# Attention followed by a gated product: the same steps in another order, with 59 visits to parts of the array instead of 84

## The chip, the cores and the metric

The kernel runs on one core of one Trainium2 chip. The time is device microseconds of one launch, the median of several runs; less is better. TensorE (PE) multiplies, VectorE (DVE), ScalarE (ACT) and GpSimd (POOL) do the element-wise work, and SyncE (SP) issues every DMA.

## The reference

Band attention with a few global tokens, followed by a gated linear layer. There are 8 batches, 8 heads, 512 local and 32 global tokens, heads 64 wide. All is float32.

```python
k_all, v_all = [k_g, k_l], [v_g, v_l]                     # joined along the tokens
out_g = sm(q_g @ k_all.T / 8) @ v_all                     # global queries see every key
s_ll  = where(abs(i - j) <= 32, q_l @ k_l.T / 8, -1e9)    # local queries: a band of 32 to each side
out_l = sm([q_l @ k_g.T / 8, s_ll]) @ v_all               # and the 32 global keys
x     = [out_g, out_l] as (8 * 544 tokens) x 512
out   = ((x @ w1) * (x @ w2)) @ w3 @ w_out                # w1, w2: 512 x 1024, w3: 1024 x 1024, w_out: 1024 x 512
```

## The kernel before

**Attention.** The work of a batch is cut into four head pairs, so there are 32 pairs m = 0 to 31, eight groups of four. For each pair the steps are: `s` (scores, line 349), 64 small matmuls that each use 64 rows and 32 columns of the array; `mm` (line 356) and `ex` (line 361), mask, minimum and exponential on DVE and ACT; the probabilities P are turned, for m < 4 by PE, for all others by DVE (line 369) with four DMAs out to DRAM (line 375) and one back in as Pt (line 380); `v` (line 399), 64 small matmuls on 128 rows and 32 columns; `nm` (line 415) divides by the sums; the result goes through PE (m < 4) or through DRAM (lines 432 and 436) into token order, and `xh` and `xl` (lines 439 and 442, the output tile is x) split it into a high and a low part in a reduced float32 type, in two halves e = 0, 1 of the tokens. The global queries of two pairs go together as one of 16 quads u: `sg` (line 466, array parts of 64 x 32), softmax, DMA out and in (Gd, Gt), `vg` (line 502, parts of 128 x 32, and line 505), `gn` (lines 510 to 512), `gb` (line 515) and so on. A step `s`, `v`, `sg` or `vg` is called a group below, and a stretch of groups between matmuls that use the whole array (128 x 128) is called a visit to parts of the array.

**Gated product.** The tokens are taken in 17 pieces k of 256, each in four quarters n. A quarter has four `first` steps (lines 548 to 550), each 12 matmuls of 128 x 256, that fill the PSUM tiles ap and bp (one buffer each); gates: `ga` copies ap to as, `gb_` (line 558) multiplies bp by it, `gh` and `gl` (lines 439 and 442, one buffer each) split the product; then two `second` steps (lines 578 to 580), each six matmuls of 128 x 512, add to acc; `out` and `store` (line 594) end a piece.

**Weights.** SP fetches w1, w2, w3 and w_out (line 650, three raw buffers); DVE and ACT unpack them (lines 606, 608, 610) and split w12 into w12h and w12l (lines 439 and 442); PE multiplies w3 by w_out in 64 `fold` steps (line 686). K and V of a pair are loaded by line 282 and lines 290 to 296; `vs` (line 305) shifts the copies of V for the first four pairs, `kc` (line 325) and `vc` (line 315) write the global keys and values into K and V.

**Order.** Nothing is scheduled at run time. A table, ORDER_OF (lines 39 to 187), holds a number for each step, and a letter A, D or P where a step may run on ACT, DVE or POOL. The steps are issued in the order of these numbers, and each engine and the one DMA queue of SP run their own in that order. An engine whose next step has to wait holds up all that stands behind it on that engine.

```python
    for n, (key, on) in enumerate(steps):
        word = next(words[key[0]])
        out.append((int(word.lstrip("ADP")), n, letters[word[0]] if word[0] in letters else on[0]))
    out.sort()
```

Of the kernel before, what the change touches and what calls it, by code (L numbers as in the profile page):

```python
# [26 lines left out]
LAG, TP, LATE, VC = 1, 4, 4, 4  # L27
# [71 lines left out]
    tp="181 179 233 236 297 300 354 357",  # L99
    pt="A186 A187 A237 A241 A302 A305 A359 A362",  # L100
    v="205 245 311 367 471 592 697 740 823 884 938 1013 1091 1127 1231 1267 1365 1403 1512 1540 1640 1677 1786  "
    "1814 1914 1951 2062 2090 2190 2225 2332 2360",
    iv="131 219 301 358 422 503 632 706 760 833 890 952 1024 1098 1188 1240 1324 1373 1463 1528 1598 1647 1737 1803  "
    "1871 1921 2011 2079 2147 2197 2284 2350",
    nm="213 249 316 376 494 628 703 750 828 887 948 1019 1094 1137 1237 1275 1369 1410 1517 1545 1643 1686 1791  "
# [953 lines left out]
```

## Time and profile before

| | |
|---|---|
| time, median of 3 runs (lowest to highest) | 813.24 us (806.35 to 817.27) |
| the profiled execution: its time, its span | 811.82 us, 810.0 us |
| mean granted clock of TensorE | 0.981 |
| PE busy with matmuls | 768.9 us (95% of the span) |
| PEld (weight loads of PE) | 668.7 us (83%) |
| DVE, ACT, POOL busy | 440.9 us (54%), 308.2 us (38%), 103.3 us (13%) |
| chain that ended last, share of the span | PE 72%, DMA 14%, DVE 6%, SP's queue 3% |
| DRAM read and written over the span | 169 GB/s |

Busy times are sums of instructions on an engine. Matmuls are pipelined, so PE's busy time tells when it had nothing to do, not how well it was used. "Granted clock" is the share of full speed at which TensorE was allowed to run. In a timeline an idle time stands in brackets, with what ended it; small matmuls of one group stand in one row.

### The profile page before, as it was taken

What the parts mean: (1) busy time and instruction counts of PE and PEld (TensorE: products, weight loads), DVE (VectorE), ACT (ScalarE), POOL (GpSimd) and SP (SyncE); (2) the same over time, 40 slices, a digit from 0 to 9 for tenths busy, and PEclk for the clock granted to TensorE, in tenths of its full rate; (3) what the DMA queues carried; (4) which work ended last, traced back from release to release, by engine and by line L of the source; (5) the groups of instructions that cost most, each with busy time, mean ns of one, the idle gap of its engine ahead of it and who ended that gap; (6) DMA issues with size and microseconds to landing.
All of it is one profiled execution on the core that took longest, in us unless ns stands there. A gap on an engine that the chain in (4) does not pass through costs nothing.

```text
span 810.0 us, 25385 instructions
## 1 busy us (share of the span) xinstructions
PE 768.9 (95%) x10564; PEld 668.7 (83%) x10564; DVE 440.9 (54%) x1371; ACT 308.2 (38%) x938; POOL 103.3 (13%) x142
## 2 busy tenths in 40 slices
PE   6799898989999999999999999999999998999995
PEld 3245587879999989999989999899989988989994
DVE  3777788757465556565645555555465655431121
ACT  2677745334344333333424242425242523211111
POOL 1121221103020011110101010101010101000000
PEclk8999999999999999999999999999999999999998
DMA  7878786868676557675756676757665567410000
GB/s 226 274 246 239 190 210 217 222 189 229 199 211 175 165 163 187 187 197 164 217 152 167 173 201 172 195 155 207 179 185 156 157 174 200 117 49 27 1 27 27
DMA packets 97467, 138.23 MB, mean 171 GB/s; under 512 B 15272, under 2 KB 57896, under 8 KB 97352
## 3 DMA queue, kind: packets, MB, share of 16 engines
q1 hardware_dynamic: 97352, 136.60, 59.7%
q8 instruction: 83, 1.36, 0.7%
q14 instruction: 32, 0.26, 0.1%
HBM read 96.71 MB, written 39.85 MB: 169 GB/s over the span
## 4 chain that ended last, share of the span: by engine, by line
PE 72%; DMA 14%; DVE 6%; SPq 3%; issue 2%; ACT 1%; POOL 1%; DVEq 0%; ACTq 0%; POOLq 0%
PE bp L548 8%; PE acc L578 7%; PE acc L579 6%; PE bp L549 6%; PE acc L580 6%; PE bp L550 6%; PE ap L548 6%; PE ap L549 6%; PE ap L550 6%; DMA Gt<-Gd 4%; PE v L399 4%; PE w L686 3%; PE s L349 3%; DMA raw_w<-in_w_t_dram 2%; PE gx L502 2%; DMA K<-in_kp_t_dram 2%
## 5 line engine op out<-in xcount | busy, mean ns | idle before, releaser
L548 PE MATMUL bp<-x,w12h 128*128 128x256 f32 x512 | 151.7, 296 | 1.2 <-DVE gl__1361 L442 0.8
L548 PE MATMUL ap<-x,w12h 128*128 128x256 f32 x512 | 146.4, 286 | 0.1
L549 PE MATMUL ap<-x,w12h 128*128 128x256 f32 x512 | 144.2, 282 | 0.0
L549 PE MATMUL bp<-x,w12h 128*128 128x256 f32 x512 | 144.2, 282 | 0.0
L550 PE MATMUL bp<-x,w12l 128*128 128x256 f32 x512 | 144.1, 281 | 0.0
L550 PE MATMUL ap<-x,w12l 128*128 128x256 f32 x512 | 143.8, 281 | 0.0
L361 ACT ACTIVATE P<-P,mn 128x128 f32<-128x128 f32 x256 | 99.7, 391 | 36.8 <-DVE mn L356 30.1
L548 PEld LDWEIGHTS bp<-x,w12h 128*128 128x128 f32 x512 | 97.7, 191 | 10.0 <-issue 5.0
L548 PEld LDWEIGHTS ap<-x,w12h 128*128 128x128 f32 x512 | 97.4, 190 | 6.9 <-issue 1.0
L549 PEld LDWEIGHTS ap<-x,w12h 128*128 128x128 f32 x512 | 97.7, 191 | 4.3
L550 PEld LDWEIGHTS ap<-x,w12l 128*128 128x128 f32 x512 | 98.3, 192 | 0.0
L550 PEld LDWEIGHTS bp<-x,w12l 128*128 128x128 f32 x512 | 97.8, 191 | 0.0
L549 PEld LDWEIGHTS bp<-x,w12h 128*128 128x128 f32 x512 | 97.6, 191 | 0.2 <-issue 0.2
L356 DVE CUSTOM_DVE_ANT_0 P<-s,cs 128x128 f32<-128x128 f32 x256 | 58.1, 285 | 31.9 <-PE s L349 31.9
L686 PE MATMUL w<-wo,w3f 128*128 128x512 f32 x128 | 63.0, 631 | 10.7 <-DVE wo L610 6.7
L315 POOL COPY V<-vg 32x1024 f32<-32x1024 f32 x40 | 44.7, 1138 | 172.0 <-PE gx L505 143.3
L686 PEld LDWEIGHTS w<-wo,w3f 128*128 128x128 f32 x128 | 23.6, 197 | 41.0 <-issue 21.8
L361 ACT ACTIVATION_READ_ACCUMULATOR P<-P,mn 128x1 f32 x256 | 48.1, 188 | 0.0
L325 POOL COPY K<-K 128x480 f32<-128x480 f32 x40 | 24.4, 616 | 173.4 <-DMA K<-in_kp_t_dram 144.6
L490 ACT ACTIVATE G<-G,mg 128x256 f32<-128x256 f32 x64 | 32.0, 501 | 34.9 <-DVE mg L484 17.5
L349 PE MATMUL s<-K,q 64*32 64x128 f32 x2048 | 38.0, 277 | 3.3 <-POOL K L325 3.0
L399 PE MATMUL v<-V,Pt 128*32 128x64 f32 x2048 | 36.2, 223 | 4.9 <-DMA Pt<-Pd 2.9
(789 smaller groups left out, 1377.4 us busy)
## 6 DMA issues: line engine op xcount, KB each, us to landing
Pd<-P SPq DMA_DIRECT2D x112, 128.0 KB
Pt<-Pd SPq DMA_DIRECT2D x28, 512.0 KB
raw_w<-in_w_t_dram SPq DMA_DIRECT2D x24, 512.0 KB
V<-in_v_t_dram SPq DMA_DIRECT2D x64, 192.0 KB
K<-in_kp_t_dram SPq DMA_DIRECT2D x36, 272.0 KB
V<-in_v_t_dram SPq DMA_DIRECT2D x36, 256.0 KB
out_dram<-o SPq DMA_DIRECT2D x34, 256.0 KB
q<-in_q_t_dram SPq DMA_DIRECT2D x32, 256.0 KB
```

The costliest lines, as they stand in the source:

```text
L315: (nc.scalar.copy if eng is nc.scalar else eng.tensor_copy)(to, src)
L349: nc.tensor.matmul(block(st[:, h], x, 128 * g), q[64 * h : 64 * h + 64, c : c + 32], window(m, h, 4 * g + x), start=True, stop=True, skip_ ...
L356: nc.vector.tensor_tensor_reduce(T["P", m][:, :, h, g], chunks(T["s", m][:, h, 128 * g : 128 * g + 128]), chunks(masks[g]), -0.125, 3.0e38 ...
L361: nc.scalar.activation(P, P, AF.Exp, bias=T["mn", m][:, g, h : h + 1], scale=-1.0, accum_out=T["sm", m][:, g, h : h + 1])
L399: nc.tensor.matmul(vt[32 * x : 32 * x + 32, g, h], t[:, x, h, g], Vs[m % NV][:, x, h, g], start=True, stop=True, skip_group_check=True)
L548: nc.tensor.matmul(d, wh[:, k, c, :], x[:, 0, 0:w], start=(k == m % 2 == 0), stop=False, skip_group_check=True)
L549: nc.tensor.matmul(d, wh[:, k, c, :], x[:, 1, 0:w], start=False, stop=False, skip_group_check=True)
L550: nc.tensor.matmul(d, wl[:, k, c, :], x[:, 0, 0:w], start=False, stop=(k == 3), skip_group_check=True)
L578: nc.tensor.matmul(a, gh[:, m % 2, sl], wh, start=(m == 0), stop=False)
L579: nc.tensor.matmul(a, gh[:, m % 2, sl], wl, start=False, stop=False)
L580: nc.tensor.matmul(a, gl[:, m % 2, sl], wh, start=False, stop=(m == 7))
L686: nc.tensor.matmul(T["w34", t], T["w3f", t, j // 4][:, j % 4], T["wo"][:, j], start=(j == 0), stop=(j == 7))
```

## The change

All of ORDER_OF is replaced; the steps and what each computes stay. A constant XT = 4 takes the place of TP = 4 in three conditions, which has no effect, as both are 4.

Counted in the order of PE, the visits to parts of the array go from 84 (72 of one group, 12 of two) to 59 (30 of one group, 21 of two, 8 of three), with the same 96 groups. A group of `v` often stands directly behind one of `s` or `sg`, and `vg` directly behind `v`. Some steps change their engine; the counts before and after are:

| step | before | after |
|---|---|---|
| w12l of the first weights (line 442, 128 x 512 and 128 x 256) | DVE 4 and 11, POOL 4 and 5 | DVE 1 and 6, POOL 7 and 10 |
| w12h (line 439, 128 x 256) | ACT 9, DVE 4, POOL 3 | ACT 6, DVE 1, POOL 9 |
| `vs`, shifts of V (line 305) | DVE 6, ACT 9, POOL 1 | DVE 2, ACT 6, POOL 8 |
| w34h (line 439); copy of turned P for m < 4 (line 439) | ACT 7, DVE 1; ACT 8 | ACT 5, DVE 3; ACT 6, DVE 2 |
| `xh`; `xl` | ACT 29, DVE 33, POOL 2; DVE 43, POOL 21 | ACT 22, DVE 19, POOL 23; DVE 32, POOL 32 |
| `ga`; `gh` | ACT 61, DVE 7; ACT 54, DVE 14 | ACT 40, DVE 28; ACT 36, DVE 32 |
| `kc`; `vc` | ACT 23, DVE 9, POOL 40; ACT 15, DVE 17, POOL 40 | ACT 33, DVE 15, POOL 24; ACT 32, DVE 13, POOL 27 |

```diff
--- before.py
+++ after.py
@@ -24,7 +24,7 @@
-LAG, TP, LATE, VC = 1, 4, 4, 4
+LAG, TP, XT, LATE, VC = 1, 4, 4, 4, 4
...
-    vs="D70 A59 A75 D76 A94 A130 D117 A138 A140 P137 D141 D136 A244 D243 A247 A250",
+    vs="A22 A90 A13 D44 P59 P203 D178 P73 A210 P166 P257 A204 P336 P356 A304 P295",
...
-    sg="507 692 810 960 1093 1229 1368 1503 1642 1778 1916 2053 2192 2324 2373 2432",
+    sg="456 632 758 901 1048 1167 1325 1448 1588 1723 1849 1999 2125 2259 2339 2409",
...
-    vg="646 770 894 1032 1160 1297 1442 1563 1716 1837 1990 2113 2263 2389 2440 2478",
+    vg="684 762 905 1049 1191 1328 1453 1636 1728 1853 2029 2180 2273 2360 2427 2469",
...
@@ -407,7 +407,7 @@
     def normalize(m):
-        if m < TP:
+        if m < XT:
...
@@ -788,7 +788,7 @@
         add(("nm", m), "DVE", [("v", m), ("iv", m)], normalize, m)
-        if m < TP:
+        if m < XT:
             take("x", 1, ("x", m), ("xt", m))
             add(("xt", m), "PE", [("nm", m), ("load", "cs")], back, m)
...
-            add(("xl", m, e), "DVE" if m < TP else "DVE POOL", [("xh", m, e)], convert, m, e, 1)
+            add(("xl", m, e), "DVE" if m < XT else "DVE POOL", [("xh", m, e)], convert, m, e, 1)
```

Three places of the order follow. The first is PE, around the global values of quad 4 (gx4) and the global scores of quad 5 (sg5); ap and bp are the tiles of `first`, acc that of `second`. Before:

```order
L550 MATMUL ap1_0_4_2777<-x1_3_0_2438,w12l5_1157 128x256
L502 MATMUL gx4_2863<-V2_79,Gt4_2754 32x64 x2
...
L505 MATMUL gx4_2863<-lg4_2595,cs_73 32x1 x4
...
L550 MATMUL ap1_1_0_3130<-x1_3_1_2457,w12l1_88 128x256
L466 MATMUL sg5_3179<-K0_75,qg2_1613 32x4x32 x16
L466 MATMUL sg5_3179<-K1_76,qg2_1613 32x4x32 x16
L548 MATMUL bp1_1_0_3216<-x1_0_1_1455,w12h0_85 128x256
```

And now:

```order
L580 MATMUL acc1_0_128_2724<-w34h3_413,gl__2823 128x512
L466 MATMUL sg5_2917<-K0_75,qg2_1263 32x4x32 x16
L466 MATMUL sg5_2917<-K1_76,qg2_1263 32x4x32 x16
L399 MATMUL v9_2954<-V0_77,Pt9_2856 32x64 x32
L502 MATMUL gx4_2987<-V2_79,Gt4_2915 32x64 x2
...
L505 MATMUL gx4_2987<-lg4_2633,cs_73 32x1 x4
L548 MATMUL bp1_0_6_3041<-x1_0_0_2054,w12h6_1115 128x256
```

sg5, v9 and gx4 now stand in one visit of three groups; gx4 stood alone ahead of sg5 before, and sg5 alone.

The second is SP's queue around the load of K for pair 8 (`K0_75<-in_kp_t_dram`). Before:

```order
L524 DMA xg_81<-gt2_1898 64x4x32
L375 DMA Pd7_1910<-P7_1649 32x4x256 x4
L594 DMA out_0_dram<-o0_0_0_1927 4x32x512
L594 DMA out_0_dram<-o0_0_128_1929 4x32x512
L282 DMA K0_75<-in_kp_t_dram 128x544
L282 DMA K1_76<-in_kp_t_dram 128x544
L432 DMA vd6_2042<-vo6_2024 32x4x128 x4
```

And now:

```order
L432 DMA vd4_1689<-vo4_1474 32x4x128 x4
L279 DMA q9_1733<-in_q_t_dram 128x512
L282 DMA K0_75<-in_kp_t_dram 128x544
L375 DMA Pd6_1791<-P6_1307 32x4x256 x4
L308 DMA vg_80<-in_vg_t_dram 32x512
L380 DMA Gt2_1847<-Gd2_1619 128x1024
L380 DMA Pt6_1851<-Pd6_1791 128x1024
```

The load was the 97th step of SP that issues DMAs, behind the first two stores of the result; it is now the 85th, ahead of pair 6's P.

The third is the work on the weights in the first part: of DVE before (numbers behind raw_w12 and w12h are the piece of the weight), of POOL now. DVE before:

```order
L610 SCALAR_TENSOR_TENSOR raw_w122_0_944<-raw_w122_0_944 128x512
L606 TENSOR_SCALAR raw_w122_1_948<-raw_w122_1_948 128x512
L610 SCALAR_TENSOR_TENSOR raw_w12s4_0_691<-raw_w12s4_0_691 128x256
L610 SCALAR_TENSOR_TENSOR raw_w122_1_948<-raw_w122_1_948 128x512
L442 TENSOR_TENSOR w12l2_90<-raw_w122_0_944,w12h2_89 128x512
L439 CAST w12h2_89<-raw_w122_1_948 128x512
L442 TENSOR_TENSOR w12l2_90<-raw_w122_1_948,w12h2_89 128x512
L606 TENSOR_SCALAR raw_w12s4_1_697<-raw_w12s4_1_697 128x256
```

POOL now:

```order
L442 TENSOR_TENSOR w12l1_88<-raw_w121_0_747,w12h1_87 128x512
L305 COPY V0_77<-V0_77 32x1536
L442 TENSOR_TENSOR w12l2_90<-raw_w122_0_882,w12h2_89 128x512
L442 TENSOR_TENSOR w12l2_90<-raw_w122_1_891,w12h2_89 128x512
L442 TENSOR_TENSOR w12l3_92<-raw_w123_0_980,w12h3_91 128x512
L442 TENSOR_TENSOR w12l3_92<-raw_w123_1_1034,w12h3_91 128x512
L439 CAST w12h4_1111<-raw_w12s4_1_651 128x256
```

The low parts of w12 pieces 2 and 3 and a shift of V, which DVE and ACT did, are in POOL's order now.

## Rows read from the trace of the kernel before

**Rows 1.** Busy time by stretch: start:end, length, busy us (instructions), granted clock PEclk, DMA share, GB/s.

```profile
0.00:180.00 180.00, 157.05 (x1899) 109.70 (x1900) 127.29 (x387) 100.14 (x275) 34.49 (x60) 0.94 0.77 225
180.00:800.00 620.00, 611.47 (x8668) 559.02 (x8666) 313.60 (x985) 207.17 (x662) 68.77 (x82) 1.00 0.56 157
```

**Rows 2.** Waits: engine, line waited for, us in total, times, longest us.

```profile
PE gx L502 <- DMA Gt<-Gd: 8.2, 6, 2.5
```

**Rows 3.** Timeline of PE, 307.7 to 320.1 us: start, duration, line, output<-inputs.

```profile
307.73 0.28 PE L549 MATMUL ap<-x,w12h 128*128 128x256 f32 x1
307.84 0.28 PE L550 MATMUL ap<-x,w12l 128*128 128x256 f32 x1
308.06 1.16 PE L349 MATMUL s<-K,q 64*32 64x128 f32 x64
309.14 0.38 PE L548 MATMUL bp<-x,w12h 128*128 128x256 f32 x1
309.36 0.28 PE L549 MATMUL bp<-x,w12h 128*128 128x256 f32 x1
...
317.71 1.16 PE L466 MATMUL sg<-K,qg 64*32 64x128 f32 x64
318.79 1.10 PE L399 MATMUL v<-V,Pt 128*32 128x64 f32 x64
319.82 0.39 PE L548 MATMUL bp<-x,w12h 128*128 128x256 f32 x1
```

**Rows 4.** Timeline of PE, ahead of the one fall of the clock after 180 us.

```profile
422.95 1.10 PE L502 MATMUL gx<-V,Gt 128*32 128x64 f32 x64 [1.82 <-DMA Gt<-Gd]
```

**Rows 5.** Busy time by stretch, columns as in the first group.

```profile
424.00:428.00 4.00, 4.00 (x32) 3.98 (x22) 3.33 (x16) 2.29 (x8) 3.25 (x3) 0.57 0.82 236
```

**Rows 6.** Waits of SP's queue, 0 to 160 us, columns as in group 2.

```profile
SPq L650 <- DVE w3f L610: 18.8, 9, 4.9
```

**Rows 7.** Busy time by stretch: the first part's middle, columns as in the first group.

```profile
40.00:160.00 120.00, 111.19 (x1553) 80.91 (x1554) 94.36 (x298) 74.77 (x216) 26.39 (x30) 0.97 0.78 223
```

**Rows 8.** Groups by line and shape: busy us, mean ns | idle before, releaser.

```profile
L442 DVE TENSOR_TENSOR w12l<-raw_w,w12h 128x512 fp32r<-128x512 f32 x4 | 2.9, 732 | 0.1
L442 DVE TENSOR_TENSOR w12l<-raw_w12s,w12h 128x256 fp32r<-128x256 f32 x11 | 4.5, 420 | 0.1
L442 POOL TENSOR_TENSOR w12l<-raw_w,w12h 128x512 fp32r<-128x512 f32 x4 | 5.2, 1309 | 12.6 <-ACT w12h L439 12.5
L442 POOL TENSOR_TENSOR w12l<-raw_w12s,w12h 128x256 fp32r<-128x256 f32 x5 | 3.7, 747 | 12.7 <-ACT w12h L439 11.8 <-DVE w12h L439 0.9
L439 POOL CAST w12h<-raw_w12s 128x256 fp32r<-128x256 f32 x3 | 1.9, 618 | 9.8 <-DVE raw_w12s L610 9.8
L305 POOL COPY V<-V 32x1536 f32<-32x1536 f32 x1 | 1.6, 1582 | 5.0 <-DMA V<-in_v_t_dram 5.0
```

**Rows 9.** The same view, forms that DVE hands on (the first without shapes apart).

```profile
L305 DVE COPY V<-V 32x384 f32<-32x384 f32 (+1 forms) x6 | 4.7, 791 | 0.9 <-DMA V<-in_v_t_dram 0.7
L439 DVE CAST w12h<-raw_w12s 128x256 fp32r<-128x256 f32 x4 | 1.2, 290 | 0.1
```

**Rows 10.** Waits of PE and DVE elsewhere, columns as in group 2.

```profile
PE s L349 <- POOL K L325: 3.0, 1, 3.0
PE v L399 <- DMA Pt<-Pd: 2.9, 2, 2.1
```

**Rows 11.** Tile x, split of the attention's result on DVE: ns min/median/max.

```profile
L442 DVE TENSOR_TENSOR x<-xr,x x35: 382/426/1146, 125.6 to 687.1; 128x256 fp32r<-128x256 f32 x35
```

**Rows 12.** Timelines of PE and DVE: the values of pair 27, its last split.

```profile
578.13 1.10 PE L399 MATMUL v<-V,Pt 128*32 128x64 f32 x64
...
592.28 0.48 DVE L442 TENSOR_TENSOR x<-xr,x 128x256 fp32r<-128x256 f32 x1 [2.08 <-ACT x L439]
```

**Rows 13.** Timeline of DVE: one gate without other work between.

```profile
794.84 0.70 DVE L558 TENSOR_TENSOR bp<-bp,as__11030 128x512 f32<-128x512 f32 x1 [3.24 <-PE bp L550]
...
796.29 0.69 DVE L442 TENSOR_TENSOR gl__11072<-bp,gh__11064 128x512 fp32r<-128x512 f32 x1
```

More of the change, by code (lines that the diff above doesn't have):

```diff
@@ L99 @@
[L99 to L105, printed above, removed]
@@ L144 @@
-    gin="2490 2494 2499 2506",
-    gxh="D2495 D2501 D2507 D2513",
-    gxl="D2496 D2502 D2509 D2514",
-    first="391 397 433 441 444 454 460 477 499 535 514 543 599 629 606 634 637 643 651 661 679 688 702 705 714 721 732  "
[12 rows of a table removed]
-    ga="D439 A465 A545 D635 D671 D693 A731 A769 A824 A856 A895 A921 A961 A996 A1034 A1059 A1092 A1130 A1152 A1195  "
[3 rows of a table removed]
-    gb_="445 486 557 642 683 711 755 809 840 876 907 943 975 1015 1049 1079 1108 1141 1178 1217 1247 1279 1315 1353  "
-    "1383 1414 1444 1490 1522 1551 1590 1628 1657 1690 1718 1765 1798 1825 1864 1902 1931 1964 1992 2040 2074  "
@@ L175 @@
-    "2596 2604",
-    second="485 491 522 528 566 570 670 686 709 717 752 763 797 804 837 844 874 886 905 914 946 955 973 984 1018 1027  "
[6 rows of a table removed]
-    out="A689 A690 A849 A851 A990 A993 D1122 D1124 A1260 A1262 A1396 A1398 A1536 A1538 D1672 D1674 A1810 A1812 D1946  "
-    "D1948 A2086 A2088 D2220 D2222 A2355 A2358 A2465 A2467 A2527 A2529 A2571 A2573 A2609 A2611",
-    store="694 695 854 857 998 1001 1125 1129 1263 1266 1399 1402 1542 1543 1675 1679 1816 1817 1949 1953 2092 2093  "
-    "2223 2227 2362 2365 2468 2473 2530 2532 2574 2576 2610 2612",
+    load="24 25 8 5 4 93 30 34 191 122 146 223 197 276 234 235 315 387 375 393 350 428 405 470 625 429 477 699 528  "
[5 rows of a table added]
@@ new lines @@
+    clear="0 1 11",
+    edges="35",
+    warm="18",
+    fetch="2 6 7 23 26 28 39 51 63 67 81 94 103 116 124 131 140 156 177 186 212 221 228 244 252 279 305 331 352 359  "
+    "398 414 64 263 358 460 463 468 490 509 514 529 540 545 568 573 587 597",
+    unit="3 9 10 12 14 17 21 15 27 37 33 38 41 40 42 46 45 48 62 52 66 72 55 74 77 83 86 87 89 91 96 92 102 112 104  "
[7 rows of a table added]
+    fold="32 65 79 101 106 143 159 160 69 82 98 107 139 141 171 173 70 75 88 97 123 144 150 167 57 71 78 108 138 145  "
+    "169 170 182 184 206 207 222 224 229 259 256 267 273 278 284 290 300 301 313 318 334 343 344 362 365 383 364  "
@@ new lines @@
+    "392 407 408 413 420 431 432",
+    w34h="D164 D200 D174 A176 A269 A342 A425 A436",
+    w34l="172 214 181 188 309 357 438 439",
+    vc="A80 A29 A95 P36 P236 P19 P209 A345 A443 P459 A520 P600 P658 A637 A687 D701 P703 P766 A846 P765 D920 A958  "
[3 rows of a table added]
+    vs="A22 A90 A13 D44 P59 P203 D178 P73 A210 P166 P257 A204 P336 P356 A304 P295",
+    kc="A16 D20 D61 D60 A153 P165 A225 P202 P262 P280 A379 A368 A501 A496 A516 A543 P657 P662 P692 P690 P805 P804  "
[3 rows of a table added]
+    s="31 99 198 243 316 399 507 576 674 734 829 865 967 1015 1107 1128 1231 1288 1367 1416 1497 1547 1633 1680  "
@@ new lines @@
+    "1754 1806 1902 1956 2028 2091 2179 2223",
+    mm="43 50 68 58 53 76 47 49 121 109 152 114 110 111 105 136 233 213 238 231 232 211 219 199 275 289 266 277 302  "
[11 rows of a table added]
+    ex="84 85 100 115 56 117 54 125 133 175 162 132 161 157 118 163 271 260 251 255 248 215 240 253 287 299 298 294  "
[11 rows of a table added]
+    tp="185 195 208 227 286 288 326 363",
+    pt="A193 A201 A230 D258 A307 D321 A366 A370",
+    v="205 282 325 385 519 620 682 733 837 904 963 1020 1115 1162 1237 1289 1365 1452 1525 1556 1635 1727 1761  "
+    "1852 1903 1961 2030 2100 2181 2276 2335 2364",
@@ new lines @@
+    iv="190 237 297 377 466 561 659 702 781 864 945 1010 1059 1127 1176 1272 1341 1392 1463 1537 1629 1668 1750  "
+    "1790 1876 1939 2021 2053 2176 2199 2291 2362",
+    nm="217 291 340 388 556 654 693 744 839 931 993 1026 1125 1174 1251 1290 1387 1460 1526 1563 1659 1738 1789  "
+    "1866 1907 1966 2052 2106 2195 2289 2353 2374",
+    xt="218 296 347 396",
+    xh="A249 A283 A308 A320 A373 A361 A401 A582 D704 P679 P761 P723 P764 D820 A791 A873 D928 P944 D985 P988 D1032  "
+    "P1078 D1070 A1187 P1212 P1242 P1274 A1286 A1300 A1349 P1326 P1351 A1539 D1483 D1569 D1575 P1576 P1639 P1604  "
@@ new lines @@
+    "P1671 P1793 D1778 D1818 P1811 P1884 D1915 D1897 A1960 D2069 P2045 A2079 P2101 D2107 D2248 A2138 D2274 A2322  "
+    "D2326 P2372 D2375 P2401 A2452 A2424 A2474",
+    xl="265 292 335 332 386 367 417 616 P739 D741 D776 D730 D775 P830 D794 P899 P990 D969 P1000 D1006 P1046 P1160  "
+    "P1077 D1207 D1247 P1255 P1291 D1312 D1324 P1444 D1334 D1356 P1550 P1522 P1585 D1591 P1582 P1729 P1616 P1703  "
+    "P1821 D1779 D1822 P1812 P1892 P1927 D1906 P2000 P2086 P2075 D2116 D2128 P2127 D2270 P2143 P2305 P2334 P2371  "
@@ new lines @@
+    "P2406 P2404 D2412 D2547 D2429 D2498",
+    tn="427 535 635 673 778 838 914 959 1055 1087 1177 1221 1327 1379 1451 1506 1573 1626 1725 1765 1869 1894 1996  "
+    "2018 2130 2183 2275 2320",
+    po="450 549 647 691 795 863 923 983 1079 1103 1185 1241 1339 1396 1482 1523 1587 1640 1726 1768 1879 1928 2007  "
+    "2048 2156 2204 2284 2342",
+    pi="478 586 668 710 809 881 941 1001 1080 1138 1209 1267 1350 1424 1489 1524 1611 1664 1742 1845 1890 1942 2014  "
+    "2062 2174 2225 2314 2354",
@@ new lines @@
+    vn="575 672 715 746 870 943 995 1027 1142 1182 1258 1295 1397 1467 1542 1568 1707 1760 1804 1871 1916 2002 2058  "
+    "2108 2198 2293 2356 2380",
+    vw="630 676 720 757 908 954 1002 1042 1148 1211 1266 1317 1420 1521 1552 1589 1717 1769 1847 1887 1951 2040  "
+    "2090 2114 2242 2315 2358 2385",
+    vi="669 717 749 787 912 981 1024 1060 1178 1226 1281 1318 1454 1553 1572 1595 1752 1796 1872 1891 1971 2066  "
+    "2092 2136 2319 2343 2384 2411",
+    sg="456 632 758 901 1048 1167 1325 1448 1588 1723 1849 1999 2125 2259 2339 2409",
@@ new lines @@
+    gm="494 499 492 486 655 638 667 639 770 777 785 780 933 903 939 919 1081 1066 1065 1072 1198 1181 1173 1180  "
+    "1345 1333 1346 1332 1476 1456 1478 1459 1614 1598 1619 1615 1743 1748 1744 1730 1854 1895 1857 1877 2020  "
+    "2010 2011 2001 2150 2139 2167 2134 2271 2268 2277 2269 2357 2363 2346 2351 2421 2420 2418 2419",
+    gr="500 686 808 940 1088 1201 1352 1480 1632 1755 1898 2039 2184 2288 2369 2423",
+    ge="546 553 584 552 694 708 695 707 831 842 833 841 948 968 975 977 1089 1108 1098 1099 1202 1233 1204 1234  "
@@ new lines @@
+    gn="711 779 922 1130 1223 1377 1492 1665 1766 1926 2084 2189 2282 2399 2428 2471",
+    gb="719 800 925 1131 1244 1399 1557 1696 1823 1940 2163 2214 2286 2414 2447 2472",
+    gc="D724 A898 D1023 D1168 A1259 D1443 D1634 A1708 A1840 A1959 A2173 A2221 D2337 D2417 A2464 A2473",
+    gd="790 906 1102 1243 1320 1479 1650 1837 1888 2065 2175 2264 2355 2450 2465 2481",
+    gin="2484 2485 2496 2509",
+    gxh="P2489 D2494 A2499 P2510",
+    gxl="P2491 D2500 D2506 D2513",
+    first="435 437 433 446 474 475 485 495 531 534 554 560 590 640 585 643 645 646 661 664 689 698 716 721 731 735 737  "
[12 rows of a table added]
@@ new lines @@
+    ga="A447 A480 A547 A641 D656 A705 D747 D796 D816 A824 A853 D894 D942 D992 A1008 A1067 A1090 D1105 A1149 A1195  "
[3 rows of a table added]
+    gb_="461 498 566 648 677 725 756 797 823 858 891 929 964 1004 1040 1071 1104 1146 1186 1213 1238 1280 1309 1342  "
+    "1372 1406 1437 1481 1512 1548 1592 1618 1666 1701 1731 1759 1798 1839 1880 1904 1937 1983 2019 2035 2085  "
+    "2131 2151 2177 2207 2250 2281 2302 2333 2386 2402 2430 2454 2478 2493 2512 2524 2534 2544 2558 2569 2582  "
+    "2591 2600",
+    gh="D462 A532 A579 D649 A683 A728 A763 A798 D832 A867 D893 A937 D965 D1013 D1047 A1074 A1106 D1163 D1190 A1214  "
[3 rows of a table added]
@@ new lines @@
+    gl="465 536 580 653 688 732 769 807 834 868 907 938 970 1014 1050 1075 1109 1169 1193 1215 1250 1287 1323 1344  "
+    "1384 1422 1462 1490 1520 1561 1597 1625 1679 1716 1737 1776 1809 1848 1886 1911 1955 1997 2027 2049 2096  "
+    "2133 2154 2182 2217 2261 2287 2316 2345 2391 2413 2440 2459 2480 2502 2518 2529 2537 2550 2561 2574 2584  "
+    "2596 2602",
+    second="504 512 562 571 622 628 660 671 697 709 752 755 782 784 812 818 850 851 888 890 918 921 953 955 979 987  "
[6 rows of a table added]
+    out="A678 A680 D819 D828 A956 A974 A1101 A1133 D1230 A1253 A1370 A1378 A1514 A1527 A1669 A1689 D1819 A1825 A1948  "
@@ L187 @@
+    "A1965 A2077 D2097 A2220 A2222 A2338 D2344 A2455 A2456 D2527 A2528 A2568 D2571 A2608 A2610",
+    store="771 860 861 871 994 1151 1210 1265 1307 1474 1447 1473 1645 1699 1741 1714 1944 1930 2034 2140 2186 2249  "
+    "2279 2267 2442 2436 2505 2483 2546 2562 2588 2606 2611 2612",
 )
```

65 lines of the change are left out of this document (5 added, 60 removed), and 128 rows, old and new, of tables (ex, first, ga, gh).

## The prediction, made before the changed kernel was run

> **What bounds the kernel now.** I read the busy times by stretch first, then what PE waits for, then its timeline, then the work beside it. In the chain that ended last PE has 72%; [rows 1] says where it loses time. From 0 to 180 us PE is busy for 157.05 us, so it stands idle for 22.95 us. From 180 to 800 us it is idle for 620 - 611.47 = 8.5 us, of which 8.2 us are waits of `vg` for Gt [rows 2]. After 180 us, then, the kernel is as long as PE's list of work, and can be shortened only where a busy PE does no work. The timeline shows such a place [rows 3]: whenever PE changes between the whole array and its parts. The first part is limited by what comes before PE, the weights and the first pairs of attention.
>
> **Fewer visits.** Whole-array matmuls of 128 x 256 start 0.11 to 0.12 us apart. In [rows 3] the first small matmul starts 0.22 us after the last whole one (308.06 - 307.84), 0.10 more than that step; the second whole one after the visit starts 0.22 us after the first (309.36 - 309.14), again 0.10 more. So a visit costs about 0.20 us beside its groups. Between two groups of different shape inside a visit nothing is saved or lost: `sg` to `v` takes 1.08 us (318.79 - 317.71), as does `s` to a whole matmul (309.14 - 308.06). The order of PE has 84 - 59 = 25 visits fewer: 25 x 0.20 = **5.0 us**. This is work of PE itself, with nothing beside it that could hide it. Ends: 4.4 us if the three of them that lie in the first part, where PE waits anyway, are worth nothing, 6.5 us if `v` and `vg`, which have the same shape and now stand together ten times, also save their joint.
>
> **The steady part (180 to 800 us).** PE's work between two steps is counted in its order, with the durations of the trace. Before, `vg` stands about 20 us behind its `sg`; now it is 34 to 41 us for all but the last two (21 and 27 us). The waits for Gt were at most 2.5 us [rows 2], so some 14 us more removes them. One of them, 1.82 us [rows 4], stands ahead of the one fall of the clock after 180 us: in 424 to 428 us the granted clock was 0.57 [rows 5], which cost 4 x (1 - 0.57) = 1.7 us and should go with it. That makes 8.5 + 1.7 = 10.2 us. The same idea applies to `s` and `v`, 19.5 us apart before and 33 or more now.
>
> What is late next? Two covers get thinner. First, `v` of the last pair of a batch to the first `first` step that reads its x: before, 16 to 25 us of PE's work lie between, now 15 to 21. For pair 27 they are four `second` and six `first` steps (about 1.4 us each, 12 matmuls at 0.117 us or six twice as wide) and one `sg`: 15.0 us. The path itself, from the end of `v` at 579.2 us to that of the last split at 592.8 us, took 13.5 us [rows 12]. So it fits with 1.5 us to spare, and any delay on DVE or POOL beyond that is a wait of PE. Second, the gate: DVE needs from 794.84 to 796.98 us, 2.1 us, for `gb_`, `gh` and `gl` [rows 13]; before, at least 6.8 us of PE's work nearly always lie between the end of bp and the `second` that reads gl, now nine quarters have only 2.7 to 2.8 us. DVE runs its list in order, so any 0.6 us of other work ahead of such a gate stops PE. In exchange ga, gh, xh and xl are spread more evenly over ACT, DVE and POOL. I keep back a third of the 10.2 us for such waits and take **6.8 us**. Ends: 10.2 us if none appears; about -3 us if each of the nine short gates costs 1 us and each of the seven batch ends 0.5 us (10.2 - 9 - 3.5).
>
> **The first part (0 to 180 us).** SP's weight fetches wait for a raw buffer that DVE has not unpacked: w3f alone stands for 18.8 us [rows 6]. DVE is busy for 94.36 of 120 us from 40 to 160 us, 79%, POOL for 26.39 us, 22% [rows 7]. The change takes work from DVE ahead of the last weight: 3 x 0.732 + 5 x 0.420 for w12l [rows 8], 3 x 0.290 for w12h and 4 x 0.791 for shifts of V [rows 9], in sum 8.3 us; it adds two w34h and two copies of Pt, 4 x 0.69 = 2.8 us, by the nearest row, a 128 x 512 split [rows 13]. That is 5.5 us less, at 79% about 7 us of DVE's time. Beside it, two waits of 3.0 and 2.9 us for K and Pt [rows 10] should mostly go, as the load of K for pair 8 now stands 12 steps earlier in SP's queue, ahead of the first stores. On the other side POOL gets 3 x 1.309 + 5 x 0.747 + 6 x 0.618 + 7 x 1.582 = 22 us more [rows 8], slow instructions on the path from a weight to PE; and it still has the room, 26 + 22 of 120 us. Also, q and V loads ahead of some weights delay these by up to 1 MB, which at the 225 GB/s of this stretch is 4.4 us [rows 1]. So the ends are 7 + 6 = 13 us less and 0 (the relief comes, but the steps that moved are late on POOL by as much). I take the middle, rounded down: **6.0 us**.
>
> **Sum.** The profiled execution took 811.8 us (the median of the runs is 0.2% above it). 811.8 - 5.0 - 6.8 - 6.0 = **794.0 us**. The end does not change: the last gate, six matmuls and the store stand as before. XT in place of TP does nothing.
>
> **Rivals.**
>
> 1. *The first part gains nothing.* POOL's slow copies replace DVE's as what weights wait for. For it: one shift takes 1582 ns on POOL, and the low part of a 128 x 512 weight 1309 ns against 732 [rows 8]. Against it: POOL's load. Then 794 + 6 = 800 us. A stronger form is contention of DVE and POOL: in [rows 11] a split of x on DVE takes 426 ns in the median and 1146 at most, so an instruction of DVE is sometimes held for about one of POOL. If all 22 us that POOL gets held DVE in the first part, the time would be 794 + 22 = 816 us. Against that, the weights' low parts took 732 and 420 ns on DVE in the mean while POOL was busy for a fifth of the time, so most of POOL's work held nothing. The Trainium skill, "SBUF — State Buffer", section "Who interferes with whom", says that a DVE instruction with two inputs in SBUF contends with a GpSimd instruction that reads SBUF; by that rule w12l, xl and their like can block each other, as the longest of those rows suggests and their median does not.
>
> 2. *Slower: the longer visits lower the clock.* There are now 29 visits of two or three groups where there were 12, so TensorE works for 2.1 to 3.2 us at a time on parts only. If each of them brought a fall like that in [rows 5], 1.7 us, this would cost 29 x 1.7 = 49 us: 843 us. It decides from 17.8 / 1.7 = 11 falls that nothing is gained, and from 21 that the kernel is slower by 2%. Against it: the clock over 180 to 800 us is 1.00 with twelve visits of two groups in the kernel, and the one fall came behind a wait [rows 1, 4]. But none of three groups exists before; if only these eight do it, 8 x 1.7 = 13.6 us, that is 807.6 us. The Trainium skill, "TensorE: Matmul & The Clock Gate", section "What's actually happening", holds that "the default state is throttled, and activity releases the throttle"; by that sentence a busy PE keeps its clock, and whether matmuls on parts of the array are activity enough no run here shows yet.
>
> 3. *All of it comes.* No new waits, and 11 us or so in the first part: 783 to 789 us.
>
> **Chances and range.** Forecast 0.57 (own range 784 to 800 us); first part without gain 0.16 (795 to 808), with full contention 0.03 (816); three-group visits lower the clock 0.10 (807.6); all longer visits do 0.06 (830 to 843); all comes 0.08. A measurement of this kernel tells about 2% from no change, 797.0 and 829.5 us. Below 797.0 lie three quarters of the forecast and all of the last case: 0.43 + 0.08 and a little of the first rival, 0.52. Slower is 0.06, and 0.42 is left. The range 782 to 811 us takes in the forecast, the first rival without contention, the three-group case and nearly all of the last; left out are 0.03 + 0.06 and the tails.
>
> **What the next profile would show.** Visits: the same 0.22 us steps, but 59 of them. Steady part: no wait of `gx` for Gt, PEclk 1.00 also in the slices with three groups, PE idle below 4 us. First part: PE idle well below 23 us, no wait of `s` for K at about 160 us, the w3f waits of SP shorter. It would be wrong if the first `first` step of a batch waits for x, if acc waits for gl, if `w` or ap wait for POOL's w12l, if DVE's w12l and x rows are stretched towards 1.1 us, or if the clock falls in the middle of the kernel.

## The result and the profile after

The changed kernel takes 782.81 us (median of 4 runs, 780.87 to 786.04) against 815.25 us, ratio 0.964 (0.955 to 0.973). The ratio is formed from mean times and leaves out one slower run of the kernel before, 819.82 us, more than 1.5% above its fastest. Later runs of the kernel before had medians of 813.2 to 814.4 us, so the gain is some 30 us. The profiled execution took 783.61 us, 28.2 us less than that of before; 17.8 us were forecast for it, with 794.0 us and a range of 782 to 811.

Busy time by stretch of the changed kernel, columns as in [rows 1]; the second stretch ends 2 us before the last matmul does:

```profile
0.00:180.00 180.00, 164.13 (x2195) 119.94 (x2196) 132.64 (x407) 102.59 (x287) 55.69 (x86) 1.00 0.81 239
180.00:771.00 591.00, 582.12 (x8365) 535.32 (x8364) 309.02 (x960) 194.01 (x626) 57.43 (x83) 1.00 0.59 160
240.00:245.00 5.00, 3.85 (x77) 3.79 (x78) 1.97 (x7) 4.06 (x20) 0.00 (x0) 0.72 0.64 194
```

In the first 180 us PE is idle for 15.87 us instead of 22.95, and its granted clock is given as 1.00 instead of 0.94. The 1.00 is too high, as two matmuls of `w` show, each the first behind other work: the one at 15 us still runs at half clock.

```profile
15.44 1.22 PE L686 MATMUL w<-wo,w3f 128*128 128x512 f32 x1
19.06 0.70 PE L686 MATMUL w<-wo,w3f 128*128 128x512 f32 x1 [0.83 <-DVE wo L610]
```

A run below that has the same first part (h1_new_start) shows its clock in 0 to 20 and 20 to 140 us as

```profile
0.00:20.00 20.00, 9.17 (x88) 6.22 (x88) 8.82 (x18) 8.98 (x11) 6.08 (x26) 0.74 0.87 277
20.00:140.00 120.00, 115.16 (x1415) 76.91 (x1415) 95.27 (x297) 80.52 (x231) 40.58 (x45) 1.00 0.78 235
```

So the falls of before at about 32, 90, 134 and 172 us are gone, but not the half clock at the start.

After 180 us PE is idle for 591 - 582.12 = 8.9 us, as much as the 8.5 us of before. What it waits for has changed (engine, line waited for: us, times, longest):

```profile
PE s L349 <- DMA q<-in_q_t_dram: 10.4, 2, 7.9
PE gx L502 <- issue: 2.5, 2, 1.5
PE v L399 <- DMA vd<-vo: 2.4, 1, 2.4
PE gx L502 <- DMA Gt<-Gd: 1.7, 2, 1.2
PE v L399 <- issue: 1.6, 1, 1.6
```

The 8.2 us of [rows 2] are 1.7 us now, but `v` and `gx` wait for other things. The timeline of PE shows a visit of three groups (206 to 210 us, with a wait in it), and the one place after 180 us where the clock fell:

```profile
205.83 1.16 PE L466 MATMUL sg<-K,qg 64*32 64x128 f32 x64
206.91 1.10 PE L399 MATMUL v<-V,Pt 128*32 128x64 f32 x64
209.23 1.10 PE L502 MATMUL gx<-V,Gt 128*32 128x64 f32 x64 [1.22 <-DMA Gt<-Gd]
...
241.15 1.10 PE L399 MATMUL v<-V,Pt 128*32 128x64 f32 x64 [2.38 <-DMA vd<-vo]
242.18 0.58 PE L548 MATMUL bp<-x,w12h 128*128 128x256 f32 x1
242.56 0.41 PE L549 MATMUL bp<-x,w12h 128*128 128x256 f32 x1
```

The fall stands behind a wait of 2.38 us, the longest of this part, and not behind a visit of three groups; whole-array matmuls of 0.41 us are those at half clock (0.28 at full).

The tile w12l shows when the weights are ready. Columns: ns min/median/max, first and last start in us. Before:

```profile
L442 DVE TENSOR_TENSOR w12l<-raw_w12s,w12h x11: 410/420/431, 106.7 to 140.8; 128x256 fp32r<-128x256 f32 x11
L442 POOL TENSOR_TENSOR w12l<-raw_w,w12h x4: 1297/1304/1331, 78.0 to 102.6; 128x512 fp32r<-128x512 f32 x4
```

The changed kernel:

```profile
L442 POOL TENSOR_TENSOR w12l<-raw_w12s,w12h x10: 738/757/1008, 96.4 to 122.4; 128x256 fp32r<-128x256 f32 x10
L442 POOL TENSOR_TENSOR w12l<-raw_w,w12h x7: 1295/1303/1315, 69.1 to 94.6; 128x512 fp32r<-128x512 f32 x7
L442 DVE TENSOR_TENSOR w12l<-raw_w12s,w12h x6: 419/426/426, 96.3 to 128.7; 128x256 fp32r<-128x256 f32 x6
```

The last low part starts at 128.7 us instead of 140.8: 12.1 us earlier, though most of them now run on POOL, where each takes nearly twice as long.

### The profile page after: what moved, and what is told of

It reads as the page before. It is cut to its first block, busy times and chain, and to the rows that moved or that the text cites. A ratio compares the mean times of both kernels' runs of the same rounds, so it can differ in the third digit from the quotient of the medians.

```text
span 781.8 us, 25358 instructions
## 1 busy us (share of the span) xinstructions
PE 748.1 (96%) x10564; PEld 656.5 (84%) x10564; DVE 441.7 (56%) x1367; ACT 297.8 (38%) x915; POOL 113.1 (14%) x169
## 4 chain that ended last, share of the span: by engine, by line
PE 80%; DMA 9%; DVE 4%; SPq 3%; issue 2%; ACT 1%; POOL 0%; DVEq 0%; ACTq 0%; POOLq 0%
PE bp L548 8%; PE acc L578 8%; PE ap L548 8%; PE bp L549 7%; PE bp L550 7%; PE acc L579 7%; PE acc L580 7%; PE ap L549 7%; PE ap L550 7%; DMA raw_w<-in_w_t_dram 4%; PE v L399 4%; PE s L349 3%; PE w L686 2%; PE gx L502 2%; PE sg L466 2%; DMA Gt<-Gd 2%
## 5 line engine op out<-in xcount | busy, mean ns | idle before, releaser
L548 PE MATMUL bp<-x,w12h 128*128 128x256 f32 x512 | 145.0, 283 | 0.7 <-DVE gl__1560 L442 0.4
L548 PE MATMUL ap<-x,w12h 128*128 128x256 f32 x512 | 144.7, 283 | 0.0
L549 PE MATMUL bp<-x,w12h 128*128 128x256 f32 x512 | 142.7, 279 | 0.0
L549 PE MATMUL ap<-x,w12h 128*128 128x256 f32 x512 | 142.2, 278 | 0.3 <-issue 0.3
L550 PE MATMUL ap<-x,w12l 128*128 128x256 f32 x512 | 142.1, 278 | 0.0
L548 PEld LDWEIGHTS ap<-x,w12h 128*128 128x128 f32 x512 | 96.3, 188 | 4.4 <-issue 2.4
L549 PEld LDWEIGHTS ap<-x,w12h 128*128 128x128 f32 x512 | 96.2, 188 | 1.5
L550 PEld LDWEIGHTS ap<-x,w12l 128*128 128x128 f32 x512 | 96.5, 188 | 0.4 <-issue 0.4
L356 DVE CUSTOM_DVE_ANT_0 P<-s,cs 128x128 f32<-128x128 f32 x256 | 62.5, 281 | 19.0 <-PE s L349 16.5
L686 PE MATMUL w<-wo,w3f 128*128 128x512 f32 x128 | 59.4, 607 | 0.8 <-DVE wo L610 0.8
L349 PE MATMUL s<-K,q 64*32 64x128 f32 x2048 | 37.8, 278 | 10.9 <-DMA q<-in_q_t_dram 10.4
L349 PEld LDWEIGHTS s<-K,q 64*32 64x32 f32 x2048 | 29.1, 107 | 18.8 <-issue 15.5
L315 ACT COPY V<-vg 32x1024 f32<-32x1024 f32 x32 | 33.3, 1045 | 24.9 <-PE gx L502 22.5
L399 PEld LDWEIGHTS v<-V,Pt 128*32 128x32 f32 x2048 | 30.3, 110 | 14.3 <-issue 5.8
```

The source lines that it names most:

```text
L315: (nc.scalar.copy if eng is nc.scalar else eng.tensor_copy)(to, src)
L349: nc.tensor.matmul(block(st[:, h], x, 128 * g), q[64 * h : 64 * h + 64, c : c + 32], window(m, h, 4 * g + x), start=True, stop=True, skip_ ...
L356: nc.vector.tensor_tensor_reduce(T["P", m][:, :, h, g], chunks(T["s", m][:, h, 128 * g : 128 * g + 128]), chunks(masks[g]), -0.125, 3.0e38 ...
L399: nc.tensor.matmul(vt[32 * x : 32 * x + 32, g, h], t[:, x, h, g], Vs[m % NV][:, x, h, g], start=True, stop=True, skip_group_check=True)
L548: nc.tensor.matmul(d, wh[:, k, c, :], x[:, 0, 0:w], start=(k == m % 2 == 0), stop=False, skip_group_check=True)
L549: nc.tensor.matmul(d, wh[:, k, c, :], x[:, 1, 0:w], start=False, stop=False, skip_group_check=True)
```

## The experiments

The edits of the table of numbers run through all of it; one entry stands for each. Ratios are to the kernel before on the same chip, where its median was 813.2 to 814.4 us; with the first result it was 815.3. The intervals reach about 4 us to each side, so two versions of the changed kernel that differ by less than some 5 us are not told apart by their times.

**First part new, the rest old.**

```diff
...
-    w34h="A178 D195 A173 A170 A234 A374 A313 A435"
+    w34h="D164 D200 D174 A176 A269 A342 A425 A436"
...
```

> The steps that make up the first 700 of the old order (to about 165 us) stand in the new order with the new engines; all later steps stand as before, with 83 to 84 visits. If the first part carries the gain (in the two traces PE's idle time from 0 to 180 us goes from 22.95 to 15.87 us and five falls of the clock there go, together 15 to 16 us), this takes 797 to 802 us, ratio to before 0.98. If the first part is worth the 6 us of the prediction, 808 us. If it only fills PE earlier and the work then waits later, 812 to 816 us.

Measured: 805.58 us, ratio 0.989 (0.986 to 0.992), with the last low part at 129.4 us. Two stretches of its trace:

```profile
0.00:140.00 140.00, 124.33 (x1503) 83.14 (x1503) 104.09 (x314) 89.50 (x242) 46.65 (x71) 0.96 0.79 241
140.00:180.00 40.00, 34.54 (x574) 31.73 (x573) 22.48 (x75) 13.14 (x45) 8.57 (x12) 0.87 0.70 202
```

Up to 140 us PE has done as many matmuls as in the changed kernel (1503 against 1499); then, in the old order, PE stands for 5.5 of 40 us, 2.3 of them in a wait of `v` for Pt and 3.0 ahead of one `s`; the changed kernel has no idle time there. The 16 us that I expected from the two traces alone were too many: 8.8 us. One of the five falls that I had counted, that of the start, is still there.

**First part old, the rest new.**

```diff
...
-    w34h="D164 D200 D174 A176 A269 A342 A425 A436"
+    w34h="A178 D195 A173 A170 A234 A374 A313 A435"
...
```

> The reverse: the first 700 steps as before, all later ones in the new order, 60 visits. If the first part carries 15 to 16 us, what is left is 24 visits at 0.20 us and a quicker pace of the whole-array matmuls, about 10 us: 803 to 807 us, ratio 0.988. If the steady part carries most, 790 to 797 us.

Measured: 794.65 us, ratio 0.978 (0.972 to 0.983). The rest carries about two thirds, 19.7 us of some 30; that is the second of the cases expected, and not the one that I had put first. Its steady part:

```profile
180.00:782.00 602.00, 597.01 (x8599) 549.13 (x8581) 316.59 (x988) 198.74 (x645) 61.36 (x88) 1.00 0.60 163
```

PE is idle for 5.0 us, against 8.5 before. With the first part new as well it is 8.9 again. That a PE that starts earlier finds more things not ready is the likely reason, and not shown apart from others.

**Every joined visit taken apart, 96 visits.**

```diff
...
-    sg="456 632 758 901 1048 1167 1325 1448 1588 1723 1849 1999 2125 2259 2339 2409"
+    sg="456 632 758 901 1048 1169 1325 1448 1588 1723 1849 1999 2125 2259 2340 2409"
...
```

> The changed kernel with every joined visit taken apart: one step of whole-array matmuls is drawn forward between two groups, so that there are 96 visits of one group. At 0.20 us for each, 37 visits more cost 7.4 us: 790 us. If a visit also sets the pace of the matmuls behind it (114 or 118 ns in both traces), another 4 to 6 us: 794 to 797 us. If visits cost nothing, 783 us.

Measured: 787.97 us, ratio 0.968 (0.965 to 0.971), 5.2 us more than the changed kernel. Its stretches:

```profile
0.00:180.00 180.00, 166.24 (x2184) 119.65 (x2185) 131.07 (x407) 102.50 (x287) 57.03 (x86) 0.96 0.79 236
180.00:771.00 591.00, 584.39 (x8359) 532.44 (x8358) 309.49 (x959) 193.57 (x625) 57.10 (x83) 1.00 0.59 161
```

Its span is 785.6 us, 3.8 more, while PE's idle time is 2.1 us less in the first stretch and 2.3 us less in the second. So PE's work grew by 8.2 us, 0.22 us for each of 37 visits: about the price of the prediction, in one execution of either kernel. The 4.4 us less of idle time are work drawn forward that fills waits.

**The old order with its visits joined, 59 visits.**

```diff
...
-    sg="507 692 810 960 1093 1229 1368 1503 1642 1778 1916 2053 2192 2324 2373 2432"
+    sg="507 692 812 960 1093 1229 1368 1504 1642 1779 1916 2054 2192 2325 2376 2434"
...
```

> The kernel before with nothing changed but that neighbouring visits are joined: up to four steps of whole-array matmuls between two visits are drawn ahead of the first, which gives 59 visits (28 of one group, 25 of two, 6 of three). At 0.20 us each, 25 fewer visits save 5.0 us: ratio 0.994, 808 to 810 us. With the pace, 9 to 10 us: ratio 0.988. If the longer visits lower the clock, or the later groups bring waits, no gain or a loss: ratio 1.00 to 1.01.

Measured: 857.76 us, ratio 1.054 (1.050 to 1.058). Waits of PE (its lines stand 8 further on than those of before):

```profile
PE gx L510 <- DMA Gt<-Gd: 19.0, 8, 6.3
...
PE bp L556 <- DVE og L518: 6.5, 2, 3.2
PE s L357 <- issue: 5.4, 2, 4.7
PE bp L556 <- DVE gl__2110 L450: 4.6, 1, 4.6
```

None of the three cases: not a gain of 5, not a small loss, but 43 us more. The count of visits is the same as in the changed kernel. By these waits, a group that is put off by up to four steps makes its DMAs and the gates behind it late, and the next visit waits. The clock fell ten times between 100 us and the end of PE's work, nine times in or right behind such a wait; its mean was 0.960 against 0.981, so up to 0.040 x 855 - 0.019 x 810 = 19 of the 43 us can be half clock. Fewer visits alone do not make the kernel faster: joined like this, their data are not there in time.

**Idle time filled, so that the clock stays up.**

```diff
+    def fill(to, n):
+        for _ in range(n):
+            nc.tensor.matmul(to, ident, ident, start=True, stop=True, skip_group_check=True)
...
+        fill(st[:, 0, 0:128], 12 * (m == 8))
...
+        fill(vt[:, 0].rearrange("p h d -> p (h d)"), 8 * (m == 5))
```

> The kernel before with 38 matmuls of 128 x 128 added that compute nothing of use: 11 ahead of the transposes of pair 3, 8 ahead of v of pair 5, 12 ahead of s of pair 8, 7 ahead of vg of quad 9, where PE stood idle for 2.8, 2.2, 3.0 and 1.8 us and the clock then fell to half. If a fall after a wait costs PE what the half clock takes (some 1.7 us each), up to four falls less give 5 to 7 us: 807 to 809 us, ratio 0.992. If the clock in the first part is covered by other waits, only the fall at 425 us counts: 812 us. If the added work delays PE more than it keeps the clock, 816 to 820 us.

Measured: 812.60 us, ratio 0.9995 (0.997 to 1.002). Three of the four falls are gone, as two stretches show that had 0.83 before:

```profile
130.00:140.00 10.00, 7.60 (x104) 6.48 (x105) 8.69 (x35) 6.57 (x23) 2.25 (x3) 1.00 0.66 199
170.00:180.00 10.00, 8.71 (x124) 8.01 (x123) 3.36 (x7) 3.12 (x10) 1.16 (x2) 1.00 0.71 216
```

The time is the same. This does not settle what the half clock costs, as one of the four fills cost time itself. Ahead of the transposes of pair 3 PE had been idle for 0.81 us, the rest of the 2.8 us lies ahead of earlier steps, and the fill (11 matmuls, 22 in the trace) took 4.35 us. Before, and with the fill:

```profile
89.72 0.84 PE L421 MATMUL xt<-cs,vo 128*128 128x128 f32 x4 [0.81 <-DVE vo L415]
```

```profile
90.20 4.35 PE L337 MATMUL xt<-cs 128*128 128x128 f32 x22
```

That is 3.5 us more. Three falls less at 1.7 us each would gain 5.1, together 1.6 us, which the interval takes in (0.997 is 2.4 us less). That the half clock in the first part is worth less than it lasts, as the next thing that PE needs comes when it comes, is possible and not shown.

**The new order with the old engines, and its reverse.**

```diff
...
-    w34h="D164 D200 D174 A176 A269 A342 A425 A436"
+    w34h="A164 D200 A174 A176 A269 A342 A425 A436"
...
```

> The new order with the old choice of engines for every step. If the new engines matter only through DVE's 5.5 us less ahead of the last weight, 787 to 790 us. If the steady part also needs them (short gates of 2.7 us, x on three engines), 795 to 805 us. If they do not matter, 783 us.

Measured: 800.05 us, ratio 0.983 (0.978 to 0.987), 17 us more than the changed kernel, as in the second case. Its last low part is as late as before:

```profile
L442 DVE TENSOR_TENSOR w12l<-raw_w12s,w12h x11: 410/418/773, 101.7 to 141.2; 128x256 fp32r<-128x256 f32 x11
```

The old order with the new engines:

```diff
...
-    w34h="A178 D195 A173 A170 A234 A374 A313 A435"
+    w34h="D178 D195 D173 A170 A234 A374 A313 A435"
...
```

> The reverse: the old order with every step on its new engine. If the engines bring the weights forward in any order, the last weight is ready at 129 to 134 us instead of 141 to 143, and with 84 visits the time is 800 to 806 us, ratio 0.985. If the engines only serve the order that they were chosen with, POOL's slow steps stand ahead of others at the wrong places and the time is 813 us or more.

Measured: 827.46 us, ratio 1.018 (1.013 to 1.023).

```profile
L442 DVE TENSOR_TENSOR w12l<-raw_w12s,w12h x6: 416/425/426, 113.5 to 149.5; 128x256 fp32r<-128x256 f32 x6
```

The order alone gives 13 us, the engines alone lose 14, both together give some 30. In the old order the new engines make the weights later, not earlier: its places for POOL's longer steps do not suit them.

**The engines in two halves: weights old, then all else old.**

```diff
...
-    pt="A193 A201 A230 D258 A307 D321 A366 A370"
+    pt="A193 A201 A230 A258 A307 A321 A366 A370"
...
```

> The changed kernel with the old engines for the weights' splits, the shifts of V, w34h and the copies of Pt alone. With the old engines everywhere the new order took 800 us and the last low part of the weights was ready at 141.6 instead of 129.1 us. If the weights are what that cost, this too has its last weight at 140 to 142 us and takes 793 to 798 us. If the weights' engines do not matter, 783 us, and the gates, x, K and V are what cost.

Measured: 791.70 us, ratio 0.973 (0.967 to 0.978), between the two cases.

```profile
L442 DVE TENSOR_TENSOR w12l<-raw_w12s,w12h x11: 415/419/426, 102.0 to 139.1; 128x256 fp32r<-128x256 f32 x11
```

```diff
...
-    gc="D724 A898 D1023 D1168 A1259 D1443 D1634 A1708 A1840 A1959 A2173 A2221 D2337 D2417 A2464 A2473"
+    gc="D724 A898 D1023 D1168 A1259 A1443 D1634 D1708 D1840 D1959 D2173 D2221 D2337 D2417 A2464 D2473"
...
```

> The other half: the weights and the shifts of V on the new engines, the gates, the splits of x, the copies into K and V and the evictions on the old ones. If the two halves add up to the 17 us and the weights cost 10 to 15, this takes 785 to 790 us, last weight at 129 to 131 us. If the short gates and the splits of x need the new engines, 793 to 798 us with waits of acc for gl or gh.

Measured: 795.49 us, ratio 0.976 (0.971 to 0.982), as in the second case.

```profile
L442 DVE TENSOR_TENSOR w12l<-raw_w12s,w12h x6: 415/422/643, 100.9 to 132.2; 128x256 fp32r<-128x256 f32 x6
```

Both halves matter, 8.9 and 12.7 us. Their sum is 4 us over the 17 of both at once, no more than the times leave open. The first makes the weights 10.4 us later. The second does so by 3.5 us and has 13.4 us of idle PE after 180 us (604 - 590.61) in place of 8.9, in waits of `v`, `gx` and, for 3.4 us, for gl:

```profile
180.00:784.00 604.00, 590.61 (x8417) 542.43 (x8417) 298.46 (x955) 199.88 (x655) 64.09 (x79) 1.00 0.59 159
```

**The kernel before once more.** No edit.

> The kernel before once more, for a second trace. If the quicker pace of the whole-array matmuls (115.0 against 116.3 ns in the mean) belongs to the order and not to the single execution, the mean is 116 to 116.5 ns again. If the falls of the clock belong to the places of the waits, they come at 31, 91, 135, 172 and 425 us again; if to chance, elsewhere, and their number is between 2 and 6.

Measured: 816.74 us, mean pace 116.1 ns. The falls after the first 20 us lie at about 89, 137, 171 and 680 us: three near the old places, the first and the last of the old ones missing, and one new. In the first 180 us PE is idle for 26.6 us here, against 22.95 in the first trace, and after that for 10.4 against 8.5: so much does one kernel vary.

**Waits of the changed kernel taken up, in two versions.** The first moves loads and the first fold too; the second only steps of whole-array matmuls.

```diff
...
-    sg="456 632 758 901 1048 1167 1325 1448 1588 1723 1849 1999 2125 2259 2339 2409"
+    sg="456 632 758 903 1048 1167 1325 1449 1588 1723 1850 1999 2125 2259 2339 2409"
...
```

> The changed kernel with the waits of its trace taken up: the masks and q of pair 0 are loaded ahead of the third weight, q of pair 1 four transfers earlier, the first fold stands ahead of s of pair 0, and one or two steps of whole-array matmuls are drawn ahead of v of pair 5, the visits that hold vg 4, 8, 9 and 11 and v of pair 11, and of the second step that waited for a gate at 592 us. If each wait costs what it lasted (11 us in the steady part with the half clock behind v of pair 11, 2 to 5 us at the start), 770 to 776 us. If the waits come back one step later, 781 to 784 us.

Measured: 787.82 us (781.50 to 789.32), ratio 0.967 (0.962 to 0.972).

```profile
PE w L686 <- DVE wo L610: 5.4, 2, 4.5
PE w L686 <- DVE w3f L610: 3.4, 1, 3.4
```

This is above both cases. `s` no longer waits for q, but the folds (`w`) wait longer for weights.

```diff
...
-    sg="456 632 758 901 1048 1167 1325 1448 1588 1723 1849 1999 2125 2259 2339 2409"
+    sg="456 632 758 903 1048 1167 1325 1448 1588 1723 1850 1999 2125 2259 2339 2409"
...
```

> The changed kernel with the start untouched and only the six steps of whole-array matmuls drawn ahead of the visits with vg 4, 9, 11 and v of pair 11 and of the second step at 592 us. If the waits of PE after 200 us can be taken away one by one, 776 to 780 us. If each comes back elsewhere, as from the earlier trial, 782 to 787 us.

Measured: 785.56 us, ratio 0.966 (0.961 to 0.971). Its waits after 190 us:

```profile
PE bp L549 <- issue: 1.9, 2, 1.6
PE acc L579 <- issue: 1.9, 1, 1.9
PE bp L548 <- DVE gl__2917 L442: 1.7, 1, 1.7
PE gx L502 <- issue: 1.7, 2, 1.0
PE v L399 <- issue: 1.7, 1, 1.7
```

The wait of `v` for 2.4 us is gone, others stand in its place. Neither version beats the changed kernel.

## Why the prediction was right, and where its steps were not

**Visits: right.** 0.20 us each was the price; taking 37 apart put 8.2 us of work on PE, 0.22 each. So 25 fewer are about the 5.0 us forecast, of PE's work. That they can be had without more waits was the rest of the change's doing, as the joined old order shows.

**Steady waits: wrong.** I took 6.8 us for waits that go. The waits for Gt went as forecast (8.2 to 1.7 us), but PE's idle time after 180 us is 8.9 instead of 8.5 us, where I had announced less than 4, and the fall of the clock at 425 us has its like at 242 us, a sign of being wrong that I had named. Nothing of the 10.2 us came, where I had kept back a third. With late weights it was 5.0 us (h2_old_start) and 5.2 us (g1_weights, 600 - 594.81):

```profile
180.00:780.00 600.00, 594.81 (x8451) 546.53 (x8449) 314.05 (x975) 197.65 (x639) 58.60 (x86) 1.00 0.59 162
```

So about 3.5 us can be had there, and the earlier start seems to use them up. With the old engines for gates and splits it is 13.4 us with early and with late weights (g2_steady; e1_letters, up to 791 us). The two covers that I named, x for the first `first` step and gl for acc, cost next to nothing: the waits in the trace are of `v` and `gx`.

**First part: the size too small, the mechanism likely right.** 6.0 us were taken, with 13 as the far end. The weights are ready 12.1 us earlier, and three runs of the new later order tell what that is worth: last low part at 128.7, 139.1 and 140.8 us give 782.8, 791.7 and 794.7 us, about 0.9 us for each us. By that the term is about 11 us, near the end of full relief; with the old order behind it the new first part gave 8.8 us for 11.4 us of earlier weights. These kernels differ in more than the last weight, in shifts of V and in w34h or in the whole first part, and no run moves the weight alone. That it is the weight which counts is the likeliest reading and not more. I had halved it because POOL's slow steps might take DVE's place. They did become what SP waits for, but shared the waiting instead of adding to it: all waits of line 650 are 69 us now, 80 before. Waits of SP, 0 to 160 us, changed kernel:

```profile
SPq L650 <- POOL w12l L442: 16.3, 11, 4.6
SPq L650 <- DVE w3f L610: 15.9, 9, 3.8
```

w3f stood at 18.8 us [rows 6], POOL's w12l at 4.9 us before. That the order alone leaves the last weight at 141.2 us, and the engines alone put it to 149.5, was not in my sum, which counted DVE's work and not which step of it stands in front of which.

**A term that was missing.** Whole-array matmuls follow each other faster: 115.0 ns in the mean against 116.3, over 6 x 512 = 3072 matmuls of 128 x 256, and 229.7 against 230.9 ns in the `second` steps, some 800: 3.9 + 1.0 = 4.9 us. Against the trace of before, 5.0 + 4.9 + 11 = 21 of the 28.2 us have a name. The other 7 us have no name. In PE's own terms the first 180 us have 7.1 us less of idle time and some 6 us less that the half clock takes: (1 - 0.94) x 180 = 10.8 us before, and (1 - 0.74) x 20 = 5.2 us for the same start in h1_new_start. These 13 us are in part the weights' 11 us under another name; how far, was not settled, and a single execution varies by 5 us. Nor need the 7 us lie in the first part: h2_old_start, which keeps the old one, gains 19.7 us, where visits and pace make 10 and its shorter idle time 3.5.

**Rivals.** *The first part gains nothing:* no. Contention of DVE and POOL did not show in the weights: the low parts on DVE take 426 ns in the median against 420 before, with POOL busy for 55.7 of 180 us instead of 34.5. By the rule of the Trainium skill, "SBUF — State Buffer", section "Who interferes with whom", they could have blocked each other. The trace agrees in four places of eight where a split of a weight or of x on DVE overlaps with work of POOL: POOL's one 128 x 256 part of 1008 ns (757 in the median) began 0.03 us after one of DVE, and three splits of x that DVE began while POOL was at work took 624, 832 and 940 ns against a median of 420. In the other four DVE's split took 434 ns at most. The one of 832, with POOL's step beside it, which ends 0.28 us before it:

```profile
408.14 0.83 DVE L442 TENSOR_TENSOR x<-xr,x 128x256 fp32r<-128x256 f32 x1
407.94 0.75 POOL L442 TENSOR_TENSOR x<-xr,x 128x256 fp32r<-128x256 f32 x1
```

In sum the three are 1.1 us of DVE, against the 22 us of this rival. *Longer visits lower the clock:* no. There are 29 of two or three groups, and the clock fell once after 180 us, behind the longest wait; the joined old order has 31, and its falls too stand by waits. This agrees with the Trainium skill, "TensorE: Matmul & The Clock Gate", section "What's actually happening", by which activity releases the throttle; small matmuls did as well as large ones here. *All of it comes:* the time is about that of this case (783 to 789 us), which had a chance of 0.08; its reason is not, as new waits did come and a quicker pace paid for them.

**The total** lay in the range and the sign was right, but the range held by 0.8 us only (782.81 us, its end at 782, one run of four below it), and the middle was 10.4 us too high for the profiled execution, under the 784 to 800 us of the forecast itself. That it held owes something to luck, as errors of both signs met. One term was 6.8 us too large, one about 5 too small, one of 4.9 was missing: 3 us between them. The other 7 are those without a name. In the first part a range from nothing to full relief was cut in half with no row that spoke for the half.

## What to carry to other kernels

Where one engine is full in the steady part, ask when the last shared input is ready, and price a new order by that moment: here each us of it went with about 0.9 us of the whole, in three kernels that differ in other things too. An order and the choice of engines belong together, so a change of one of them is not to be priced by the other's busy time: apart they gave 13 us and lost 14, together they gave some 30. And a wait in a trace is not a gain to be had: in two trials the waits that were taken away had others in their place. Look also at the first matmuls of a trace before the granted clock of its first stretch is believed.
